# An output product in 64x64 TensorE quadrants, with single scores in a new plan

## The chip, the cores and the metric

One core of a Trainium2 chip. The metric is the device time of one execution in microseconds (us); "before" and "changed" are medians of several runs of the same rounds.

## The reference, cut to what matters

Attention with normalised q and k over 8 batches, 12 heads, 448 tokens and head size 64; then a feed-forward layer on the 3584 tokens.

```python
q_n, k_n = rmsnorm(q, g_q), rmsnorm(k, g_k)
attn = softmax(q_n @ k_n.T / 8)                 # per batch and head
x = (attn @ v) as 3584 x 768
h = x @ w_in                                    # 768 -> 2048
g = h + sin(alpha * h) ** 2 / alpha
out = g @ w_out                                 # 2048 -> 768
```

## The kernel before

Each batch b has a stage: its 21 score tiles (S), the attention of its 6 head pairs (A), and, as filler for TensorE (F), the output product of batch b - 1. A stage ends with the first product (x @ w_in, tile `hps`), which fills g_sb. Stages 1 to 7 are the ones with fillers. `ops`, `sc`, `av` and `hps` are PSUM tiles; there are four *bank pairs*, and all of them share these.

```python
def bank_pair(name, dtype=F32):          # one of four slots of two PSUM banks
    slot = min(free_at, key=free_at.get) # the slot that a rough clock expects first
    ...
def second_product(b):
    ...
    units = [[(i, half) for half in range(2)] for i in order]   # one row tile: both halves of 768 columns
    ...                                                         # batch 0 and odd batches differ: cut here
    for unit in units:
        def step(m, unit=unit, st=st):
            if m == 0:
                st["ps"] = bank_pair("ops")
            for k, (i, half) in enumerate(unit):
                ...                                             # c0: first column of this row tile
                nc.tensor.matmul(st["ps"][:, k, :HALF], g_sb[:, m, c0:c0 + P],          # 128x128
                                 w_out_sb[:, m, half * HALF:(half + 1) * HALF], start=(m == 0), stop=(m == MT - 1))
            if m == MT - 1:
                nc.vector.tensor_copy(osb[:, :n], st["ps"][:, :n, :HALF])
                ...                                                                    # store
# ... one stage:
PLAN = "6 SS 7 SS 7 SSS 8 SSS 8 SSAS 7 SS 5 SSASA 4 S 4 SSAAA"    # 6 fillers, 2 scores, 7 fillers, ...
SLOTS = 24                                  # the plan's 83 entries in 24 slots
at[2] += [lambda: begin_norm(n3), step_of(n3, 0, 1, 2)]            # next batch's norm: squares on GpSimd
at[10] += [lambda: begin_norm(n4), step_of(n4, 0, 1)]
for slot, task in ((10, step_of(n3, 3)), (11, step_of(n3, 4)),     # two sums on VectorE (reduce)
                   (12, step_of(n3, 5)), (12, step_of(n4, 2)),     # inverse root on ScalarE, then scaling
                   (13, step_of(n4, 3)), (15, step_of(n4, 4)), (17, step_of(n3, 6)), (18, step_of(n4, 5)),
                   (23, step_of(n4, 6))):
    at[slot].append(task)
```

`attend` (A) ends with a logarithm and an exponential on ScalarE (tile `rec`) and two VectorE multiplies into `xT`, which give its bank pair back. Scores give theirs back after ScalarE's exponential (`expT`). An output unit gives its pair back after VectorE's copy into `osb`.

Of the kernel before, what the change touches and what calls it, by code (L numbers as in the profile page):

```python
# [23 lines left out]
F32 = mybir.dt.float32  # L24
# [8 lines left out]
def kernel(  # L33
# [23 lines left out]
    nc = tc.nc  # L57
    B, H, S, D = q.shape
    D_MODEL = H * D
    D_FF = moe_w_in.shape[1]  # L60
    P = 128
    KT = D_MODEL // P
    MT = D_FF // P
    NP = H // 2
    NT = S // P
    REST = S - NT * P
    NJ = S // REST
# [3 lines left out]
    HALF = D_MODEL // 2  # L71
# [16 lines left out]
    opool = ctx.enter_context(tc.tile_pool(name="osb", bufs=3))  # L88
# [8 lines left out]
    def bank_pair(name, dtype=F32):  # L97
        slot = min(free_at, key=free_at.get)
        clock["pe"] = max(clock["pe"], free_at.pop(slot))
        ps = psum.tile([P, 2, 2048 // mybir.dt.size(dtype)], dtype, tag=f"ps{slot}", name=name)  # L100
        slot_of[id(ps)] = slot
        return ps

    def passes(pe=0.0, act=0.0):

        clock["pe"] += pe
        if act:
            clock["act"] = max(clock["act"], clock["pe"] + 0.25) + act
        return max(clock["pe"], clock["act"] if act else 0.0)

    def give_back(ps, time):
        free_at[slot_of.pop(id(ps))] = time
# [48 lines left out]
    w_out_sb = wpool.tile([P, MT, D_MODEL], BF16)  # L161
    g_sb = gpool.tile([P, MT, 2 * S], BF16)
# [222 lines left out]
    def second_product(b):  # L385


        steps = []
        odd = b % 2
        rows = [out[c * S:(c + 1) * S, :].rearrange("(p j) d -> j p d", j=NJ) for c in range(B)]  # L390
        order = [NT] * odd + list(range(NT))

        units = [[(i, half) for half in range(2)] for i in order]
        if b == 0:
            units = [[(i, half) for i in rows_] for half in range(2) for rows_ in (order[:2], order[2:])]
        if odd:
            units[-1:] = [[x] for x in units[-1]]
        for unit in units:
            st = {}

            def step(m, unit=unit, st=st):
                if m == 0:
                    st["ps"] = bank_pair("ops")
                for k, (i, half) in enumerate(unit):
                    c0 = odd * (S + REST) + i * P if i < NT else NT * P
                    nc.tensor.matmul(st["ps"][:, k, :HALF], g_sb[:, m, c0:c0 + P],  # L406
                                     w_out_sb[:, m, half * HALF:(half + 1) * HALF], start=(m == 0), stop=(m == MT - 1))
                passes(0.163 * len(unit))
                if m == MT - 1:
                    n = len(unit)  # L410
                    osb = opool.tile([P, 2, HALF], F32, tag="osb", name="osb")
                    nc.vector.tensor_copy(osb[:, :n], st["ps"][:, :n, :HALF])  # L412
                    give_back(st["ps"], passes() + 1.2)
                    whole = n == 2 and unit[0][0] == unit[1][0]
                    for k, (i, half) in enumerate(unit[:1] if whole else unit):
                        src = osb.rearrange("p a d -> p (a d)") if whole else osb[:, k]
                        cols = slice(0, D_MODEL) if whole else slice(half * HALF, (half + 1) * HALF)
                        for jj in range(2):
                            dst = rows[b][odd + 2 * i + jj] if i < NT else rows[b - 1 + jj][(NJ - 1) * (1 - jj)]
                            eng = nc.scalar if b == B - 1 and jj else nc.sync  # L420
                            eng.dma_start(out=dst[:, cols], in_=src[jj * 64:jj * 64 + 64, :])
            each = 2 // len(unit)
            steps += [lambda m=m, s=step, e=each: [s(m * e + x) for x in range(e)] for m in range(MT // each)]
        return steps
# [9 lines left out]
    c0, c1 = norm[0], norm[1]  # L434
# [108 lines left out]
    first_product(0, beside)  # L543


    PLAN = "6 SS 7 SS 7 SSS 8 SSS 8 SSAS 7 SS 5 SSASA 4 S 4 SSAAA"
    KEPT, SLOTS = MT // 2, 24
    plan = [x for word in PLAN.split() for x in ("F" * int(word) if word.isdigit() else word)]
    for b in range(1, B):
        nc.scalar.preload_act_table_set(EXP_LN)  # L550
        clock["act"] = clock["pe"] + 3.3
        fillers.extendleft(reversed(second_product(b - 1)))

        n_fill = len(fillers) - (KEPT if b % 2 == 0 else 0)
# [30 lines left out]
    for s in second_product(B - 1):  # L585
        s()
# [28 lines left out]
```

## Time and profile before

| | before |
|---|---|
| time | 434.88 us |
| TensorE busy | 98% |
| ScalarE, GpSimd, VectorE busy | 78%, 64%, 53% |
| stage 1 (from the end of hps to the next hps) | 30.44 us |
| stages 2 to 7, each | 32.02 us |

A "stage" below is always the stretch from the modelled end of one batch's hps matmuls to the start of the next batch's. It is the best yardstick here: stages 2 to 6 of a kernel agree within 0.03 us where the clock is the same, while the time to the first hps differs between runs (38.2 to 41.3 us, with how many half-clock stretches fall in it).

### The profile page before, as it was taken

The numbers are of one execution on the slowest core, as the hardware profiler recorded it, in microseconds if no ns is written. First come the engines' busy times: TensorE is split into PE (matmuls) and PEld (weight loads), VectorE is DVE, ScalarE is ACT, GpSimd is POOL, SyncE is SP. The second block draws the span as 40 slices with busy tenths as digits, with TensorE's granted clock in tenths as the row PEclk, the third lists the DMA queues.
The fourth block names the chain that finished last, engine by engine and source line by source line (L and its number), as shares of the span: only waits on it lengthen the run. The fifth ranks groups of instructions, "written<-read, shape, count | busy, mean of one in ns | idle before, by whom it ended". The sixth has DMA issues, their size and how long they took to land.

```text
span 434.6 us, 9514 instructions
## 1 busy us (share of the span) xinstructions
PE 423.9 (98%) x3844; PEld 220.5 (51%) x3844; DVE 231.6 (53%) x335; ACT 338.4 (78%) x529; POOL 279.7 (64%) x263
## 2 busy tenths in 40 slices
PE   7889999999999999999999999999999999999996
PEld 3335554555455555555555555555555555555563
DVE  4778564557455564547453564464645474246511
ACT  4889789878888787878879788887878788788600
POOL 4969789936995659927798369947599176002300
PEclk9989999999999999999999999999999999999999
DMA  7999999690249505692067903494063901320022
GB/s 254 209 257 206 215 192 231 143 267 15 67 151 217 144 0 131 121 223 100 10 193 180 194 1 82 150 221 125 1 196 85 126 1 33 84 57 2 0 67 79
DMA packets 68240, 54.63 MB, mean 126 GB/s; under 512 B 39636, under 2 KB 63972, under 8 KB 68196
## 3 DMA queue, kind: packets, MB, share of 16 engines
q1 hardware_dynamic: 54834, 40.51, 36.1%
q0 software_dynamic: 12416, 11.81, 18.0%
q10 hardware_dynamic: 946, 1.70, 1.0%
q8 instruction: 30, 0.49, 0.5%
q14 instruction: 14, 0.11, 0.1%
HBM read 45.62 MB, written 11.01 MB: 130 GB/s over the span
## 4 chain that ended last, share of the span: by engine, by line
PE 82%; DVE 1%; ACT 1%; POOL 0%; issue 0%; POOLq 0%
PE ops L406 32%; PE hps L353 29%; PE av L314 13%; PE sc L294 7%; ACT expT L297 1%; DVE ms L227 0%; POOL sq L221 0%; DVE osb L412 0%; DVE g_sb L340 0%; DVE xT L326 0%; ACT inv L236 0%; ACT inv L237 0%; POOLq L246 0%
## 5 line engine op out<-in xcount | busy, mean ns | idle before, releaser
L297 ACT ACTIVATE expT<-sc 128x896 bf16<-128x896 f32 x168 | 144.7, 914 | 30.6 <-PE sc L294 29.5
L406 PE MATMUL ops<-w_out_sb,g_sb 128*128 128x384 bf16 x896 | 156.6, 327 | 0.0
L353 PE MATMUL hps<-xT,w_in 128*128 128x448 bf16 x768 | 146.8, 353 | 0.0
L335 POOL TENSOR_TENSOR s<-s 128x448 f32<-128x448 f32 x64 | 59.5, 934 | 114.4 <-ACT s L332 100.8
L406 PEld LDWEIGHTS <-g_sb 128*128 128x128 bf16 x896 | 83.1, 98 | 70.0 <-issue 18.8
L340 DVE SCALAR_TENSOR_TENSOR g_sb<-s,inv_alpha_sb,hps 128x448 bf16<-128x448 f32 x128 | 80.8, 676 | 60.9 <-POOL s L335 60.9
L353 PEld LDWEIGHTS <-w_in 128*128 128x128 bf16 x768 | 74.4, 98 | 71.4 <-issue 2.9
L332 ACT ACTIVATE s<-hps,alpha_sb 128x448 f32<-128x448 f32 x128 | 74.6, 628 | 28.3 <-PE hps L353 26.5
L326 DVE TENSOR_TENSOR xT<-av,rec 64x448 bf16<-64x448 f32 x96 | 59.7, 622 | 50.1 <-ACT rec L321 30.8
L246 POOL TENSOR_TENSOR qkn<-qk,inv 128x448 bf16<-128x448 f32 x80 | 72.7, 939 | 7.4 <-POOL qk L224 7.0
L221 POOL TENSOR_TENSOR sq<-qk 128x896 f32<-128x896 f32 x44 | 73.4, 1685 | 0.0
L314 PE MATMUL av<-expT,vb 64*64 64x448 bf16 x672 | 70.6, 352 | 0.6 <-DVE osb L412 0.3
L314 PE MATMUL av<-expT,ones 64*64 64x448 bf16 x672 | 70.7, 352 | 0.0
L227 DVE TENSOR_REDUCE ms<-sq 128x14 f32<-128x896 f32 x44 | 47.5, 1083 | 25.0 <-POOL sq L221 24.7
L412 DVE COPY osb<-ops 128x768 f32<-128x768 f32 (+1 forms) x33 | 27.6, 837 | 51.4 <-PE ops L406 45.5
L294 PE MATMUL sc<-qkT 64*64 64x448 bf16 x672 | 51.3, 362 | 2.5 <-DVE qkT L276 1.4
L224 POOL TENSOR_TENSOR qk<-qk,gg 128x896 f32<-128x896 f32 x24 | 50.2, 2094 | 1.8 <-ACT gg L171 1.8
L314 PEld LDWEIGHTS <-vb 64*64 64x64 bf16 x672 | 37.6, 107 | 12.5 <-issue 1.1
L314 PEld LDWEIGHTS <-ones 64*64 64x64 bf16 x672 | 37.4, 107 | 11.3
L337 ACT ACTIVATE s<-s 128x448 f32<-128x448 f32 x64 | 36.9, 577 | 2.8
L294 PEld LDWEIGHTS <-qkT 64*64 64x64 bf16 x672 | 15.1, 105 | 30.6 <-issue 26.4
L321 ACT ACTIVATE rec<-rec 128x448 f32<-128x448 f32 x48 | 27.7, 577 | 1.5
(44 smaller groups left out, 138.6 us busy)
## 6 DMA issues: line engine op xcount, KB each, us to landing
qk<-in_q_dram SPq DMA_DIRECT2D x24, 448.0 KB, 4.8
qk<-in_k_dram SPq DMA_DIRECT2D x22, 448.0 KB, 4.8
out_dram<-osb SPq DMA_DIRECT2D x39, 192.0 KB, 2.8
vb<-in_v_dram POOLq DMA_DIRECT2D x32, 168.0 KB, 6.4
w_in<-in_moe_w_in_dram POOLq DMA_DIRECT2D x4, 768.0 KB, 11.9
w_out_sb<-in_moe_w_out_dram POOLq DMA_DIRECT2D x2, 1536.0 KB, 24.2
out_dram<-osb SPq DMA_DIRECT2D x26, 96.0 KB, 4.5
qk<-in_k_dram ACTq DMA_DIRECT2D x2, 448.0 KB, 6.0
```

The source lines that it names most:

```text
L221: nc.gpsimd.tensor_mul(st.sq[w], qk[ci][:, w], qk[ci][:, w])
L224: eng.tensor_mul(qk[ci][:, 0], qk[ci][:, 0], gg.to_broadcast([P, 2 * NJ, D]))
L246: eng.tensor_mul(n[:, :, hi, :], x[:, hi], inv[:, hi].unsqueeze(2).to_broadcast([P, NJ, D]))
L294: nc.tensor.matmul(sc[key_rows(pp, hi), pp, :S], qkt[r, 1, j * REST:(j + 1) * REST], qkt[r, 0, :], start=True, stop=True)
L297: nc.scalar.activation(expT[c, j], sc[:, :, :S], ACT.Exp, scale=SCALE)
L314: nc.tensor.matmul(av[o, part, :S], ones[r, :] if part else vb[b][r, hp, j, :], expT[pi // 2, j][r, pi % 2, :], start=(j == 0), stop=(j == ...
L326: nc.vector.tensor_mul(xT[b][r, hp, :], av[r, 0, :S], rec[o, :])
L332: nc.scalar.activation(s1, hps, ACT.Sin, scale=alpha_sb[:, m, :])
L335: nc.gpsimd.tensor_mul(s2, s1, s1)
L340: nc.vector.scalar_tensor_tensor(g_sb[:, m, (b % 2) * S:(b % 2 + 1) * S], s2, inv_alpha_sb[:, m, :], hps, op0=ALU.mult, op1=ALU.add)
L353: nc.tensor.matmul(ps[:, m % 2, :S], w_in_sb[m * 2 // MT][:, kt, m % (MT // 2) * P:(m % (MT // 2) + 1) * P], x[:, kt, :], start=(kt == 0), ...
L406: nc.tensor.matmul(st["ps"][:, k, :HALF], g_sb[:, m, c0:c0 + P], w_out_sb[:, m, half * HALF:(half + 1) * HALF], start=(m == 0), stop=(m == ...
```

## The change

Its intent: run the output product in 64x64 quadrants, the shape of scores and attention, so that TensorE does not change shape within a stage; then scores need not be bunched. A quadrant contracts 64 rows, so each output exists as two halves in two banks: VectorE copies one and adds the other. A unit is now one half of the columns of a row tile, and it takes a whole bank pair, as a unit of both halves did before. Batch 7's product stays as it was.

```diff
-        units = [[(i, half) for half in range(2)] for i in order]
+            units = [[(i, half)] for i in order for half in range(2)]       # batches 1 to 6; batch 0 half by half
...
+            def quadrants(m, unit=unit, st=st):
+                for r in range(2):
+                    for o in range(2):
+                        rs, os = slice(r * 64, r * 64 + 64), slice(o * 64, o * 64 + 64)
+                        nc.tensor.matmul(st["ps"][os, r, :HALF], g_sb[rs, m, c0 + o * 64:c0 + o * 64 + 64],
+                                         w_out_sb[rs, m, half * HALF:(half + 1) * HALF], start=(m == 0), stop=(m == MT - 1))
+                if m == MT - 1:
+                    nc.vector.tensor_copy(osb[:, 0], st["ps"][:, 0, :HALF])
+                    nc.vector.tensor_add(osb[:, 0], osb[:, 0], st["ps"][:, 1, :HALF])
...
+            step = whole_array if b == B - 1 else quadrants
...
-    PLAN = "6 SS 7 SS 7 SSS 8 SSS 8 SSAS 7 SS 5 SSASA 4 S 4 SSAAA"
+    PLAN = "6 S 4 S 2 S 2 S 2 S 2 S 2 SS 2 S 2 A 1 S A 3 S 2 S 2 S 2 S 1 S 1 S 4 S A S A 3 S 2 S 5 S 4 AA 2"
```

More of the change, by code (lines that the diff above doesn't have):

```diff
@@ L391, in second_product, with store, whole_array @@
         order = [NT] * odd + list(range(NT))
-        units = [[(i, half) for half in range(2)] for i in order]
-        if b == 0:
-            units = [[(i, half) for i in rows_] for half in range(2) for rows_ in (order[:2], order[2:])]
-        if odd:
-            units[-1:] = [[x] for x in units[-1]]
+        if b == B - 1:
+            units = [[(i, half) for half in range(2)] for i in order[:-1]] + [[(order[-1], half)] for half in range(2)]
+        elif b == 0:
+            units = [[(i, half)] for half in range(2) for i in order]
+        else:
+            units = [[(i, half)] for i in order for half in range(2)]
+        osbs = {}
+        def store(osb, i, cols):
+            for jj in range(2):
+                dst = rows[b][odd + 2 * i + jj] if i < NT else rows[b - 1 + jj][(NJ - 1) * (1 - jj)]
+                eng = nc.scalar if b == B - 1 and jj else nc.sync
+                eng.dma_start(out=dst[:, cols], in_=osb[jj * 64:jj * 64 + 64].rearrange("p a d -> p (a d)"))
         for unit in units:
             st = {}
-            def step(m, unit=unit, st=st):
+            def whole_array(m, unit=unit, st=st):
                 if m == 0:
@@ L409, in step @@
                 if m == MT - 1:
-                    n = len(unit)
+                    n, i = len(unit), unit[0][0]
                     osb = opool.tile([P, 2, HALF], F32, tag="osb", name="osb")
@@ L413, in step @@
                     give_back(st["ps"], passes() + 1.2)
-                    whole = n == 2 and unit[0][0] == unit[1][0]
-                    for k, (i, half) in enumerate(unit[:1] if whole else unit):
-                        src = osb.rearrange("p a d -> p (a d)") if whole else osb[:, k]
-                        cols = slice(0, D_MODEL) if whole else slice(half * HALF, (half + 1) * HALF)
-                        for jj in range(2):
-                            dst = rows[b][odd + 2 * i + jj] if i < NT else rows[b - 1 + jj][(NJ - 1) * (1 - jj)]
-                            eng = nc.scalar if b == B - 1 and jj else nc.sync
-                            eng.dma_start(out=dst[:, cols], in_=src[jj * 64:jj * 64 + 64, :])
+                    store(osb[:, :n], i, slice(unit[0][1] * HALF, (unit[-1][1] + 1) * HALF))
+            def quadrants(m, unit=unit, st=st):
+                (i, half), = unit
+                if m == 0:
+                    st["ps"] = bank_pair("ops")
+                c0 = odd * (S + REST) + i * P if i < NT else NT * P
+                for r in range(2):
[3 more added lines that the diff above has]
+                                         w_out_sb[rs, m, half * HALF:(half + 1) * HALF], start=(m == 0), stop=(m == MT - 1))
+                passes(0.163)
+                if m == MT - 1:
+                    if half == 0 or b == 0:
+                        osbs[i] = opool.tile([P, 2, HALF], F32, tag="osb", name="osb")
+                    osb = osbs[i][:, half:half + 1]
+                    nc.vector.tensor_copy(osb[:, 0], st["ps"][:, 0, :HALF])
+                    nc.vector.tensor_add(osb[:, 0], osb[:, 0], st["ps"][:, 1, :HALF])
+                    give_back(st["ps"], passes() + 1.6)
+                    apart = b == 0 or (odd and i == order[-1])
+                    if apart:
+                        store(osb, i, slice(half * HALF, (half + 1) * HALF))
+                    elif half:
+                        store(osbs[i], i, slice(0, D_MODEL))
+            step = whole_array if b == B - 1 else quadrants
             each = 2 // len(unit)
```

## The prediction

> **What bounds the kernel now.** I read the page's busy shares and its chain first, then the chain in order of time, the stretches of one batch, and the timelines of ScalarE, VectorE and GpSimd inside one attention stage.
>
> ```profile
> PE 423.9 (98%) x3844; PEld 220.5 (51%) x3844; DVE 231.6 (53%) x335; ACT 338.4 (78%) x529; POOL 279.7 (64%) x263
> PEclk9989999999999999999999999999999999999999
> PE 82%; DVE 1%; ACT 1%; POOL 0%; issue 0%; POOLq 0%
> ```
>
> TensorE is busy nearly always, at full clock, and 82% of the chain that ended last is TensorE work. A busy TensorE is not a TensorE at its best, though, so the chain in order of time comes next. This is the attention stage of batch 2, with the products around it:
>
> ```profile
> 107.71 1.95 PE ops L406 x12
> 109.66 0.50 PE sc L294 x8
> 110.16 2.38 PE ops L406 x14
> 112.54 0.50 PE sc L294 x8
> 113.04 2.38 PE ops L406 x14
> 115.42 0.69 PE sc L294 x12
> 116.11 2.71 PE ops L406 x16
> ...
> 122.72 1.32 PE av L314 x28
> 124.04 0.19 PE sc L294 x4
> 124.23 2.38 PE ops L406 x14
> ...
> 135.82 3.97 PE av L314 x84
> 139.79 18.27 PE hps L353 x96
> ...
> 409.82 20.81 PE ops L406 x128
> ```
>
> The last line gives the price of the output product alone: 20.81 us / 128 = 0.1626 us a pass (384 columns). Two lines above it, av in 64x64 quadrants, four matmuls together, takes 3.97 us / 21 groups = 0.189 us a group (448 columns). A whole-array pass of the same 448 columns (hps) takes 18.27 / 96 = 0.190. So four quadrants together cost what one whole pass costs. A score group (4 quadrant matmuls) between two av groups takes 0.19. But between output passes two score groups take 0.50 and not 0.38, and 14 output passes take 2.38 and not 2.28. Each excursion from 128x128 to 64x64 and back costs about 0.12 + 0.10 us.
>
> The sum confirms it. The stage from 107.7 to 139.8 lasts 32.1 us and holds 112 output passes, 21 score groups and 42 av groups: 112 x 0.1626 + 63 x 0.189 = 18.21 + 11.91 = 30.12. What is over is 1.98 us. The plan has nine runs of output passes, each followed by scores or attention, so nine round trips: **0.22 us a round trip**, with nothing left for waits. In these stages TensorE never waits; its only waste is the change of shape.
>
> Next, what stands close behind TensorE:
>
> ```profile
> 107.70:139.80 32.10, 32.10 (x366) 16.83 (x364) 15.83 (x22) 27.43 (x41) 26.96 (x24) 1.00 0.53 137
> 139.80:158.06 18.26, 18.26 (x98) 9.43 (x99) 11.41 (x18) 14.31 (x24) 9.69 (x9) 1.00 0.44 103
> ```
>
> The columns after the span are TensorE, weight load, VectorE, ScalarE, GpSimd. In the stage ScalarE works 27.4 of 32.1 us: second bound, 4.7 us of slack. GpSimd 27.0, VectorE 15.8.
>
> ```profile
> L297 ACT ACTIVATE expT<-sc 128x896 bf16<-128x896 f32 x168 | 144.7, 914 | 30.6 <-PE sc L294 29.5
> L412 DVE COPY osb<-ops 128x384 f32<-128x384 f32 x10 | 5.6, 558 | 8.1 <-PE ops L406 8.0
> L412 DVE COPY osb<-ops 128x768 f32<-128x768 f32 x23 | 22.0, 958 | 43.3 <-PE ops L406 37.4 <-DMA qkT<-qkn 5.8
> ```
>
> The exponentials wait for scores, 29.5 us in all, and not the other way round.
>
> [...]
>
> **The change part by part.**
> Removed: the shape change between output passes, scores and attention. In each of the seven stages (batches 1 to 7, which carry the output products of batches 0 to 6) nine round trips become one, from and to hps. Gain 8 x 0.22 = 1.77 us a stage, 12.4 us over seven.
>
> Added on TensorE: the 768 whole passes of batches 0 to 6 become 3072 quadrant matmuls, with as many weight loads. A group of four should cost 384 columns as one pass does, 0.1626 us, by the av comparison. Two things could spoil that. A quadrant's weight load lasts 107 ns, which still fits under a 160 ns stream. Eight instructions in 162 ns are 20 ns each; av does eight in 189 (24 ns), and the PE transposes of the first stage do 224 instructions in 3.6 us (16 ns each). So neither binds. [...]
>
> Added on VectorE: per row tile, two copies and two adds of 384 columns in place of one copy of 768. A copy is 0.558; the add I estimate at 0.56 from the same size (the xT multiply of 448 columns is 0.62). That is 4 x 0.56 - 0.96 = 1.3 us, times 24 row tiles = 31 us more on VectorE, 232 to 263 of about 425. In the stage some 16 + 4.5 = 20.5 of 30 us: beside TensorE, not in its way, except that a bank pair comes back after 1.2 us and not 1.0, and there are twice as many bank pairs (7 units a stage, not 3.5) out of four.
>
> Moved: the scores, from bunches of two and three to singles every two filler steps (0.65 + 0.19 = 0.84 us). ScalarE takes an exponential every 0.80 us when they follow each other (three in 2.51 us in its timeline). So TensorE now offers them at the rate ScalarE can take. I walked the plan by hand with F = 0.325, S = 0.189, A = 1.323 us from the stage's start; ScalarE is free for the first exponential at 3.1 us (table load and sines before it, 110.82 - 107.7). Scores 5 to 9 are issued at 6.1, 6.9, 7.8, 7.9 and 8.8; exponentials 3 to 7 end at 6.2, 7.0, 7.8, 8.6 and 9.4, each giving a slot back. With one pair for the running output unit and one being drained after the 16th step (until about 7.4 us), score 6 waits about 0.15 us and the next unit's first step 0.05. The walk finds similar crumbs at the later unit ends (24, 32, 48), about 0.3 us in all. ScalarE ends its last exponential near 26.7 us and the last reciprocal at 30.7, while TensorE ends at 30.3. Both are nearly level, so **I charge 0.3 us a stage for waits**.
>
> The first stage is another matter: it lasts 31.7 us with only 96 output passes (15.6 + 11.9 + 2.0 = 29.5 expected), because VectorE stands behind late squares on GpSimd (sq at 72.9 to 76.2, VectorE idle 2.6 us before its sum) and attention waits for xT. That wait of 2.2 us is not of the shape change, and the new plan reaches the same point no later. I give this stage 1.2 us of gain, not 1.77.
>
> Sum: 434.75 - 6 x (1.77 - 0.3) - 1.2 = 424.7, which I round to **424.6 us**, 2.3% less.
>
> **The rivals.** (a) *ScalarE becomes the bound.* Its 27.4 us of work must fit in 30.35, after a start 3.1 us late; GpSimd and VectorE feed its small inverses. For it: the walk shows ScalarE busy without a gap from 3.1 to 14 us. Against: it idles 29.5 us before exponentials now. If each stage lost 1 us to it, the time would be 434.75 - 12.4 + 7 = 429.4, within 2%. (b) *Bank pairs come back late.* VectorE works in order: a copy stands behind a multiply that waits for a reciprocal (2 to 3 us of VectorE idle at three such places in the stage), and now twice as many units depend on it. If two of the seven units in a stage cost 0.4 us each: 428. (c) *A quadrant group costs more than a pass* (weight loads of the same row half, row halves in two banks). At 170 ns the loss is 7.5 ns x 768 = 5.8 us, and the time 430. Against it stands av. (d) *Nothing is lost*: no waits, and the first stage gains fully: 422.4; if the first stage also loses its old wait, 420.5.
>
> **Range and chances.** The floor is (d), 421 to 422; (a), (b) and (c) reach 428 to 430, and I don't expect two of them at once. Range 421.8 to 429.0. The border of 2% lies at 426.1, 1.5 us above my number, that is 0.2 us a stage. So faster 0.66, within 2% 0.31, slower 0.03; slower would need a new wait of 3 us in every stage.
>
> **What would show it right or wrong.** In the chain in order of time, score groups between output groups should take 0.19 and not 0.25 to 0.31, and output groups 0.162. The stage between two hps runs should be 30.4 to 30.8 us (32.1 now), the first 30.5. VectorE busy should be about 263 us, ScalarE's idle before expT well below 29.5. If TensorE shows waits for ScalarE (score slots) or for VectorE (output slots) of more than 0.5 us a stage, rival (a) or (b) has it; if output groups take 170 ns without waits, (c). The prediction is wrong at its root if the stage keeps 32 us although the round trips are gone.

That the halves need a copy and then an add, and not one instruction, is not shown here; it is how the change is written.

## The result

Before 434.88 us, changed 450.18 us (449.24 to 452.53). The ratio is 1.036 (95% interval 1.033 to 1.039): slower by 3.6%. Ratios are the mean time of one kernel's fast runs over that of the other's of the same rounds, so not quite the ratio of the medians quoted. The profiled run took 452.53 us, the slowest of the five, at a granted clock of 0.98; the others had 0.985 to 0.989, so its stages hold more of the half clock told of below than those of the median run.

The page of the changed kernel:

```profile
PE 425.1 (94%) x6148; PEld 264.1 (59%) x6148; DVE 259.6 (58%) x403; ACT 338.2 (75%) x529; POOL 280.0 (62%) x263
PEclk9889999999989999899999999999998999999999
```

TensorE, busy 98% before, now waits, and its clock is below full speed in several slices. But the quadrants themselves do as predicted. The chain in order of time, stage 2, first lines:

```profile
117.65 0.65 PE ops L435 x16
118.30 0.19 PE sc L294 x4
```

Sixteen quadrant matmuls, four groups, take 0.65 us, 0.1625 each (0.1626 for a whole pass before), and a score group between them takes 0.19 (0.25 before). The shape change is gone. A copy takes 556 ns and an add 554, as estimated. So the loss is in waits. The stages of the changed kernel, of batches 2, 4 and 7, in windows set by hand that are up to 0.04 us longer than the stages in the table below (span, TensorE, weight load, VectorE, ScalarE, GpSimd; then the granted clock):

```profile
113.36:148.20 34.84, 32.69 (x702) 24.17 (x702) 19.44 (x31) 28.05 (x42) 27.02 (x24) 0.95 0.52 117
219.94:253.40 33.46, 31.21 (x702) 23.08 (x702) 19.45 (x31) 27.84 (x42) 27.02 (x24) 1.00 0.46 122
376.89:407.70 30.81, 30.57 (x702) 22.44 (x702) 15.30 (x27) 26.98 (x38) 6.60 (x6) 1.00 0.29 56
```

The last stage carries the same quadrants and the same plan and is 1.2 us shorter than before (30.77 against 32.02). What it lacks is the norm of a next batch: four sums on VectorE (31 to 27 instructions) and GpSimd's work for them. The other stages are longer than before, and those in which the clock fell are longer by another 1.4 to 1.7 us (34.8 to 35.1 against 33.4). Here is the chain in stage 2 where it leaves TensorE:

```profile
123.53 1.35 PE av L314 x27
...
129.78 1.10 DVE ms L227
...
130.90 0.33 ACT inv L236
...
131.48 0.81 ACT expT L297
...
132.33 0.56 PE sc L294 x4
132.89 0.64 PE ops L435 x8
```

A score group waits for an exponential (a bank pair), which stands behind the norm's inverse on ScalarE, which waits for a sum on VectorE. The last line shows the clock: eight quadrant matmuls take 0.64 us and not 0.33. VectorE in the same stretch, the changed kernel:

```profile
126.09 1.26 DVE L326 TENSOR_TENSOR xT<-av,rec 64x448 bf16<-64x448 f32 x2 [1.37 <-ACT rec L321]
127.38 1.08 DVE L227 TENSOR_REDUCE ms<-sq 128x14 f32<-128x896 f32 x1
128.50 1.25 DVE L326 TENSOR_TENSOR xT<-av,rec 64x448 bf16<-64x448 f32 x2
129.78 2.08 DVE L227 TENSOR_REDUCE ms<-sq 128x14 f32<-128x896 f32 x2
131.89 0.56 DVE L442 COPY osb<-ops 128x384 f32<-128x384 f32 x1
132.48 0.55 DVE L443 TENSOR_TENSOR osb<-osb,ops 128x384 f32<-128x384 f32 x1
```

and the kernel before, at the same place in its stage 2:

```profile
117.78 1.09 DVE L227 TENSOR_REDUCE ms<-sq 128x14 f32<-128x896 f32 x1 [2.67 <-POOL sq L221]
119.42 1.09 DVE L227 TENSOR_REDUCE ms<-sq 128x14 f32<-128x896 f32 x1 [0.56 <-POOL sq L221]
120.95 0.96 DVE L412 COPY osb<-ops 128x768 f32<-128x768 f32 x1 [0.44 <-PE ops L406]
123.12 1.08 DVE L227 TENSOR_REDUCE ms<-sq 128x14 f32<-128x896 f32 x1 [1.20 <-POOL sq L221]
125.39 1.26 DVE L326 TENSOR_TENSOR xT<-av,rec 64x448 bf16<-64x448 f32 x2 [1.18 <-ACT rec L321]
```

Before, three of the sums stand ahead of the first multiplies into xT, with idle time of VectorE around them. In the new plan the multiplies of pair 0, which wait for a reciprocal, stand ahead of all three, and those of pair 1 ahead of the last two; sums, multiplies, copy and add form one chain of 6.9 us without a gap (126.09 to 133.0), and three bank pairs hang on it. (The profile puts 12 us of VectorE's idle time before copies down to stores of `osb`. One such copy, at 123.58, began 0.05 us after the last matmul of its unit, 122.88 + 0.65, so no store held it up.)

### The profile page after: what moved, and what is told of

It reads as the page before. It is cut to its first block, busy times and chain, and to the rows that moved or that the text cites. A ratio compares the mean times of both kernels' runs of the same rounds, so it can differ in the third digit from the quotient of the medians.

```text
span 450.8 us, 14156 instructions
## 1 busy us (share of the span) xinstructions
PE 425.1 (94%) x6148; PEld 264.1 (59%) x6148; DVE 259.6 (58%) x403; ACT 338.2 (75%) x529; POOL 280.0 (62%) x263
## 4 chain that ended last, share of the span: by engine, by line
PE 64%; DVE 9%; ACT 7%; POOL 3%; issue 2%; POOLq 0%
PE hps L353 25%; PE ops L435 19%; PE av L314 10%; PE sc L294 5%; PE ops L415 5%; ACT expT L297 4%; DVE ms L227 3%; DVE g_sb L340 3%; DVE xT L326 3%; POOL s L335 3%; ACT rec L321 1%; ACT rec L320 1%; ACT s L332 1%; ACT inv L236 0%; ACT inv L237 0%
## 5 line engine op out<-in xcount | busy, mean ns | idle before, releaser
L435 PE MATMUL ops<-w_out_sb,g_sb 64*64 64x384 bf16 x3072 | 161.2, 330 | 3.5 <-DVE g_sb L340 1.7
L435 PEld LDWEIGHTS <-g_sb 64*64 64x64 bf16 x3072 | 104.2, 109 | 40.6 <-issue 6.4
L294 PE MATMUL sc<-qkT 64*64 64x448 bf16 x672 | 68.3, 363 | 14.6 <-ACT expT L297 9.8
L314 PE MATMUL av<-expT,vb 64*64 64x448 bf16 x672 | 73.3, 354 | 0.7 <-ACT expT L297 0.4
L314 PE MATMUL av<-expT,ones 64*64 64x448 bf16 x672 | 73.0, 354 | 0.0
L442 DVE COPY osb<-ops 128x384 f32<-128x384 f32 x48 | 26.7, 556 | 41.6 <-PE ops L435 29.1
L314 PEld LDWEIGHTS <-vb 64*64 64x64 bf16 x672 | 42.0, 109 | 9.1 <-issue 1.3
L314 PEld LDWEIGHTS <-ones 64*64 64x64 bf16 x672 | 41.8, 109 | 7.9
L294 PEld LDWEIGHTS <-qkT 64*64 64x64 bf16 x672 | 26.7, 108 | 30.8 <-issue 22.4
L320 ACT ACTIVATE rec<-av 128x448 f32<-128x448 f32 x48 | 26.0, 541 | 20.8 <-PE av L314 20.5
```

What stands on the lines that cost most here:

```text
L294: nc.tensor.matmul(sc[key_rows(pp, hi), pp, :S], qkt[r, 1, j * REST:(j + 1) * REST], qkt[r, 0, :], start=True, stop=True)
L314: nc.tensor.matmul(av[o, part, :S], ones[r, :] if part else vb[b][r, hp, j, :], expT[pi // 2, j][r, pi % 2, :], start=(j == 0), stop=(j == ...
L435: nc.tensor.matmul(st["ps"][os, r, :HALF], g_sb[rs, m, c0 + o * 64:c0 + o * 64 + 64], w_out_sb[rs, m, half * HALF:(half + 1) * HALF], star ...
```

## The experiments

Stages in us, from the profiled run, and the median time of all runs; a profiled run lies up to 2.4 us from its median. "h" marks values that hold a stretch at half clock.

| kernel | stage 1 | stages 2 to 6 | stage 7 | time |
|---|---|---|---|---|
| before | 30.44 | 32.02 | 32.02 | 434.88 |
| changed | 34.43 | 33.42; 34.8 to 35.1 h | 30.77 | 450.18 |
| quad_old_plan | 33.49 | 31.29 | 30.81 | 433.68 |
| whole_new_plan | 37.07 h | 35.99 | 34.80 | 464.33 |
| sums_early | 33.39 | 31.88 | 30.77 | 436.03 |
| two_units | 35.87 h | 33.94; 35.6 h | 31.26 | 455.48 |
| quad_old_sum16 | 33.44 | 31.18 | 30.81 | 433.23 |
| quad_old_no_add | 31.80 | 30.73 | 30.73 | 429.68 |
| inv_late | 36.74 h | 32.87 | 30.76 | 444.07 |
| quad_1to6_sum16 | 30.44 | 31.18 | 30.80 | 431.03 |
| new_no_add | 36.01 | 33.45; 35.0 h | 30.77 | 447.93 |
| sums_no_add | 32.76 | 31.30 | 30.76 | 433.63 |
| first_unit_m13 | 30.44 | 31.18 | 30.81 | 431.10 |
| first_tile_whole | 31.47 | 31.80 | 31.42 | 435.69 |

The kernel before took 435.09 us beside the first four, 436.15 beside the next four (434.9 to 436.5) and 434.92 beside the last four.

**One part each: the plan or the quadrants.**

```diff
# quad_old_plan, from the changed kernel        # whole_new_plan, from the kernel before
-    PLAN = "6 S 4 S 2 S ..."                   -    PLAN = "6 SS 7 SS ..."
+    PLAN = "6 SS 7 SS ..."                     +    PLAN = "6 S 4 S 2 S ..."
```

> The quadrants kept, the plan of before put back. Theory A (the quadrants do what was predicted, the new plan's order does the harm: it puts the attention of pairs 0 and 1 ahead of the sums of the next batch's norm, VectorE reaches the sums late, ScalarE stands in its inverse and TensorE runs out of score slots): 424 to 428 us, every stage near 30.5 to 31 us, with at most 0.5 us of wait for g_sb at a stage's start. Rival B (the quadrants do the harm: twice as many bank pairs and 31 us more of VectorE): 440 us or more, the stage stays at 33 or above.

> The kernel before with the new plan alone: whole-array output product, 21 runs of output passes a stage and not 9. The shape changes alone cost 12 x 0.22 = 2.6 us a stage, 18 us in all: 453 us. Theory A adds the wait behind the sums, 1.5 to 3 us in six stages: 462 to 471 us, with ScalarE waiting about 2 us a stage for the sums before its inverse. Rival B: no such wait, 453 us.

quad_old_plan: 433.68 us, ratio 0.997 (0.994 to 0.999). whole_new_plan: 464.33 us, ratio 1.067 (1.064 to 1.070). The first falls between the two theories: the plan does most of the harm, but the quadrants do not give 424 either. The second is theory A's number, and its stages tell how it is made up. In stage 7, without sums, it is 34.80 - 32.02 = 2.78 us longer than before: twelve more round trips at 0.23. In stages 2 to 6 it is 3.97 longer, so there 1.2 us more are of the plan's order. With quadrants the order costs 33.42 - 31.29 = 2.1 us in stages 2 to 6 and nothing in stage 7 (30.77 against 30.81). So where there is no next norm, single scores cost nothing. Rival (a) of the prediction, ScalarE as the bound, finds no support there; sums_no_add below tests it with the norm present.

What is left in quad_old_plan is VectorE again, smaller. Its stage 2, VectorE and then the chain:

```profile
127.87 1.09 DVE L227 TENSOR_REDUCE ms<-sq 128x14 f32<-128x896 f32 x1
128.99 0.56 DVE L442 COPY osb<-ops 128x384 f32<-128x384 f32 x1
129.58 0.55 DVE L443 TENSOR_TENSOR osb<-osb,ops 128x384 f32<-128x384 f32 x1
```

```profile
129.58 0.56 DVE osb L443
...
130.18 0.57 PE sc L294 x8
```

A score waits 0.5 us for an output unit's bank pair, because the sum stands ahead of the copy. Stage 1 lost 3.05 us, most of it at such places (TensorE waits there four times for an add: 0.7, 0.7, 1.6 and 0.8 us).

**The sums ahead of the multiplies.**

```diff
+        sums = {33: step_of(n3, 3), 36: step_of(n3, 4)} if b + 1 < B else {}   # entries of the plan, just ahead of A, A
-            for slot, task in ((10, step_of(n3, 3)), (11, step_of(n3, 4)), (12, step_of(n3, 5)), ...
+            for slot, task in ((12, step_of(n3, 5)), ...
```

> The changed kernel with two sums of the norm moved on VectorE: the first just ahead of the attention of pair 0, the second just ahead of that of pair 1. Theory A: ScalarE's wait for the sums (2.1 us a stage) and TensorE's waits of 0.6 and 1.9 us and the half clock after them go: stage near 31 us, 428 to 432 us in all. Rival B: nothing moves, 448 us or more. Rival C (ScalarE can't follow single scores anyway): the wait moves elsewhere, 440 to 446 us.

436.03 us, ratio to before 1.002 (1.000 to 1.004): 14 us less than the changed kernel with two sums moved, and no half clock in any stage. Stages 2 to 6 fell from 33.42 to 31.88 us without half clock, which makes 7.7 us for the five; stage 1 gave 1.0, and most of the rest is the half clock that no longer comes. Theory A's direction, but its 31 us and 428 to 432 were not reached. VectorE, stage 2 of this run:

```profile
123.35 1.09 DVE L227 TENSOR_REDUCE ms<-sq 128x14 f32<-128x896 f32 x1
124.47 1.26 DVE L326 TENSOR_TENSOR xT<-av,rec 64x448 bf16<-64x448 f32 x2
125.76 1.08 DVE L227 TENSOR_REDUCE ms<-sq 128x14 f32<-128x896 f32 x1
126.87 0.56 DVE L442 COPY osb<-ops 128x384 f32<-128x384 f32 x1
```

One of the sums now stands ahead of the first multiplies (at 120.61, they at 122.06), so that one fewer stands between these and the copy; the rest of the chain is still there.

**Whether ScalarE's standing is enough.**

```diff
-                               (11, step_of(n3, 4)), (12, step_of(n3, 5)), ...
+                               (11, step_of(n3, 4)), (14, step_of(n3, 5)), ...       # the inverse two slots later
```

> The changed kernel with the norm's inverse of the next batch's first group moved on ScalarE to two slots later, the sums on VectorE left where they are. If ScalarE, standing in that inverse for the sums, is what starves TensorE: ScalarE's 2.1 us go, stage 31.5 us or less, 432 to 437 us. If VectorE holding the output unit's and the attention's bank pairs is enough by itself: stage 33 us or more, 442 us or more.

444.07 us, ratio 1.019 (1.016 to 1.022): 6 us less than the changed kernel. ScalarE's wait for the sum fell from 2.1 to 0.4 us a stage, but the stage fell only from 33.42 to 32.87, 2.8 us over five stages; most of the rest goes with the half clock, which in the profiled run fell in stage 1 alone. The chain of this run now leaves TensorE for VectorE alone:

```profile
129.04 2.08 DVE ms L227 x2
...
131.15 0.57 DVE osb L442
...
131.74 0.56 DVE osb L443
...
132.35 0.38 PE sc L294 x4
```

So ScalarE standing in the inverse is the last link, not the cause: without it the same score waits 1.6 us for the output unit's pair. The cause is the place of the sums in VectorE's order. (The limit of 33 us that I had set for this case was missed by 0.13.)

**VectorE's added work.** The add left out, wrong results on purpose:

```diff
-                    nc.vector.tensor_add(osb[:, 0], osb[:, 0], st["ps"][:, 1, :HALF])
```

> Quadrants with the old plan, the add of the second bank left out (the result is wrong on purpose): VectorE has 27 us less, and each bank pair comes back 0.58 us earlier. Theory A: the wait of 0.47 us in stages 2 to 6 goes (2.4 us), and of the 3.05 us that the first stage lost some 1.5 to 2: 429 to 430 us. If VectorE's added work does not matter: 433.7 us.

> The changed kernel with the add of the second bank left out (wrong on purpose): VectorE 27 us less, each output bank pair back 0.58 us earlier. If the order of the sums in the new plan does its harm by itself, the wait behind them stays: stages of 32.2 to 32.9 us without the half clock, 441 to 447 us. If the harm is only VectorE's added time: 436 us or less.

> The new plan with the two sums moved ahead (436.0 us, stages of 31.87) and the add left out as well (wrong on purpose). If the rest over the ideal stage is VectorE's added time plus 0.45 us for g_sb at the start: stages of 30.8 us, 429 to 431 us, as quadrants with the old plan and no add (429.7). If single scores cost something of their own: 433 us or more.

With the old plan 429.68 us, ratio 0.986 (0.983 to 0.988): stages 2 to 6 at 30.73, the same as stage 7, and stage 1 down by 1.7. With the new plan as it is 447.93, and 33.45 us against 33.42: nothing gained. (Its first stage even grew, from 34.43 to 36.01 us: a score there waits 1.9 us, until 68.57, for a transposed q and k from DMA, `qkT<-qkn`, a wait that the changed kernel does not have. Why this transfer came late was not followed.) With the sums moved 433.63 us, 31.30 against 31.88. So the add costs 0.56 to 0.58 us a stage where the order is good, and is hidden behind the sums where the order is bad. The expectation for the last run, 30.8, was missed, and its 433.63 us fall under "single scores cost something of their own". Its trace says otherwise. In stage 4 an output unit waits 0.48 us for the bank pair of the early multiplies, where in quad_old_no_add a score waits 0.21 behind these multiplies, and the start waits 0.43 us for g_sb against 0.29; no wait for an exponential is over 0.08 us. These make 0.5 of the 0.57 us between 31.30 and 30.73. So the rest is again the early attention in VectorE's order, and not ScalarE. (These waits are counted from the steady pace of the matmuls, 0.0406 us a quadrant of output; by the same count the changed kernel has 0.48 and 0.43 us at the two places.)

**The start of a stage.** The changed kernel wants g_sb of m 14 after 14 groups, half as late as before; it waits 0.47 us at 116 us. Two ways to take that away. In two_units the first two units run abreast; in first_unit_m13, built on the fastest version, the first unit reads older rows. Its output is wrong, which doesn't matter for the time.

```diff
# two_units, from the changed kernel
+            steps[:16] = steps[:7] + steps[8:15] + [steps[7], steps[15]]
# first_unit_m13, from quad_1to6_sum16
+                gm = m - 2 if first and m > 13 else m       # g_sb[rs, gm, ...]
```

> The changed kernel with the first two output units of a stage run abreast, so that the last two k-steps (g_sb of m 14 and 15) are wanted after 28 groups and not after 14. Theory A says that only the 0.5 to 0.8 us at each stage's start goes: 3 to 6 us less than the changed kernel, 444 to 447 us. If the wait at the start is what puts the later waits where they are, 435 us or less.

> The fastest version so far (431.0 us), the first output unit of a stage taking m 12 and 13 of g_sb again in place of 14 and 15 (wrong on purpose), so that it does not wait for the end of the first product's tail. If the wait at the start is worth its 0.45 us: six stages 31.18 to 30.73, 428.3 us. If the time comes back in later waits for bank pairs: 431 us.

two_units: 455.48 us, ratio 1.046 (1.044 to 1.049) where the changed kernel had 1.036: slower still, and both expectations missed. Two pairs for output units at once leave two for scores: in its stage 3 TensorE waits 0.4 and 0.6 us for exponentials at the start, and the later waits (0.5 and 1.9 us) are all still there. first_unit_m13: 431.10 us, stages of 31.18 us as without it. The first unit no longer stops for g_sb, which had cost 0.29 us in quad_1to6_sum16 and not the 0.45 expected. But the second unit then waits 0.16 us, put down to the same last instruction of g_sb, and a score behind it 0.24 us and not 0.09, its weight load for the first unit's add. So the gain was not to be had: bank pairs, by the trace, are what is short.

**Versions meant to be faster.**

```diff
# quad_old_sum16, from quad_old_plan: one sum after the copy and the add
-                               (13, step_of(n4, 3)), (15, step_of(n4, 4)), ...
+                               (13, step_of(n4, 3)), (16, step_of(n4, 4)), ...
# quad_1to6_sum16: the same, and batch 0 on the whole array with its units and stores of before
+            step = whole_array if b in (0, B - 1) else quadrants
# first_tile_whole, from quad_1to6_sum16: first row tile of each stage on the whole array
+            units = [[(order[0], half) for half in range(2)]] + [[(i, half)] for i in order[1:] for half in range(2)]
+    PLAN = "8 SSS 8 SS 6 SS 6 SSS 8 SSAS 7 SS 5 SSASA 4 S 4 SSAAA"
```

> Quadrants with the old plan (433.7 us, stages of 31.29 us), one sum of the norm moved on VectorE from ahead of an output unit's copy and add to after it. Theory A (bank pairs come back late because VectorE, in order, has sums and multiplies ahead of the copy and the add): TensorE's wait of 0.47 us for the add in each of five stages goes, stages of 30.8 us, 431.2 us. Rival D (the wait is only of the added VectorE time, wherever it stands): 433.7 us still.

> A version meant to be faster than both: the output product of batch 0 as in the kernel before (whole array, in the first stage, which lost 3.05 us with quadrants), quadrants for batches 1 to 6, the old plan, and the sum moved as in the run beside it. Theory A: first stage 30.4, stages 2 to 7 at 30.8 us: 434.9 - 6 x 1.2 = 427.7 us, 427 to 429. If the first stage's loss is not of the quadrants: 430 us or more.

> The same version with the first row tile of every stage on the whole array (both halves abreast, m 14 wanted after 28 passes) and the scores of the first words set so that only one more round trip of 0.22 us is paid. No wait for g_sb (0.45 us less), 1.3 us less of VectorE: stages of 30.6 to 31.0 us, 427 to 430 us. If the start is tight for another reason, 431 us or more.

quad_old_sum16: the long wait for the add is gone, but the stage gained only 0.11 us of the 0.5, and 433.23 us is nearer to rival D than to theory A. Two waits appeared elsewhere: 0.3 us at the last three A and 0.07 at a score. quad_1to6_sum16: 431.03 us, ratio 0.988 (0.986 to 0.991), correct, faster than both kernels, though by less than the 2% that count as faster here. The 427 to 429 us expected were not reached, since stages 2 to 6 stayed at 31.18. Its first two stages:

```profile
57.73:88.17 30.44, 29.82 (x349) 15.73 (x347) 15.28 (x21) 27.24 (x41) 28.01 (x25) 1.00 0.99 206
106.50:137.68 31.18, 31.07 (x702) 22.07 (x701) 19.74 (x32) 27.43 (x41) 26.97 (x24) 1.00 0.56 137
```

The first stage is back at 30.44, so all of its 3.05 us were of the quadrants there, with the units and stores that go with them (the moved sum alone left 33.44 in quad_old_sum16). first_tile_whole failed: 435.69 us and 31.80 us a stage. It pays one more round trip of 0.22 us and bunches three scores at the start; in its stage 4 the output unit after the first five scores waits 0.6 us (until 216.07) for the bank pair of an exponential.

## Why the prediction was wrong

The price list was right: 0.22 us a round trip (whole_new_plan: 0.23), 0.1625 us a quadrant group, 0.55 us a copy or an add, VectorE 259.6 us busy (263 said). Rivals (a) and (c), which it held for less likely, did not come true. Where nothing else happens, in stage 7, the walk's 30.4 to 30.8 us came out: 30.77.

**The step that failed is "I charge 0.3 us a stage for waits"**, and the hand walk behind it. The walk followed TensorE and ScalarE and gave VectorE a fixed 1.2 us per bank pair. VectorE kept to the order of the program here: it stood idle for 1.37 us until 126.09 for the reciprocal, though the squares of two sums had been done at 125.04, and the first of these sums came behind the multiplies, at 127.38 us; from 126.09 to 133.0 us each instruction ran behind the other. The walk did not ask what the two early A put in front of the sums of slots 10 and 11. Measured in their place, stage 4, without half clock, against 30.6 said: about 2.9 us of waits more. The gaps between TensorE's matmuls in stage 2, which has the same ones, are 0.47 us (g_sb at the start), 0.59 (an output unit for a bank pair that the multiplies hold) and 1.88 (a score behind the sum and the inverse).

**Rival (b) came closest, and was sized at 428.** It had the engine and its order right, but named only multiplies that wait for reciprocals, not the sums behind them. It was written as "If two of the seven units in a stage cost 0.4 us each"; the waits in stage 2 cost 0.59 and 1.88 us. Nor did it count what a bank pair carries: a unit of one half of the columns (384) now holds the pair that two halves (768) shared, until a copy and an add of 0.556 + 0.554 us, where one copy of 0.958 us had freed it.

**The clock was left out.** The 1.88 us of idle TensorE, which came 0.65 us of work after the 0.59, was followed in three of five stages of the profiled run by 3.4 us at a granted clock of 0.5, worth 1.4 to 1.7 us each: 4.8 us. The forecast had no term for it. Why three and not five? In the traces of both kernels all changes of the granted clock lie on a grid of 3.41 us (in the changed kernel half clock from 132.42 to 135.83, 187.03 to 190.44 and 344.04 to 347.46). The stretches of this grid just before the half clock had 1.5 to 1.6 us of matmuls (stages 2, 3 and 6). In stages 4 and 5 a border of the grid cut the same idle time in two, and no stretch had under 2.0 us. This is a hint and no rule: a stretch of stage 1 with 1.5 us was followed by full clock.

**"The new plan reaches the same point no later" for stage 1** failed too: 4.0 us longer than before and not 1.2 shorter. Quadrants with the old plan lose 3.05 of it; quad_1to6_sum16 gets it back. That stage has 48 fillers and not 56 between its scores, so that its pairs are probably wanted sooner; this was not tested. The prediction had also misread the stage: 31.7 us with a wait of 2.2. By the yardstick here it took 30.44 us, with two waits of 0.5 us (until 66.31 and 79.13), so there was less to gain. (Smaller slips: in the stage of batch 2 VectorE idles for over 2 us before multiplies at two places, 2.17 and 2.57 us, not at three; 434.75 - 12.4 - 2.2 is 420.2, not 420.5. They change nothing.)

The sum for the profiled run: stage 1 5.2 us over the prediction, stages 2 to 6 together 19.1 (5 of it the clock), stage 7 0.2, and 1.7 before the first hps, where two stretches of half clock fell and one in the kernel before.

Settled is that the order of the sums makes this a loss: with two of them moved the time is that of the kernel before (sums_early, 1.002). It does not bring the gain; the new plan with the sums moved is still 11 us over the prediction. Settled too is that leaving out the add saves about 0.57 us a stage where the order is not in the way. Open are why stage 1 suffers more than the others, and why the late transfer in new_no_add was late.

## What to carry to other kernels

When a plan is rearranged, write down the order of work of every engine, not only of the bound one: a task that keeps its place in the plan changes its place in an engine's work when something else moves across it (here the sums, behind multiplies that waited until 126.09 us). Splitting the contraction over row halves halved what a PSUM bank pair carries here (384 columns and not 768); with four pairs for everything, count how long each is held before counting what the bound engine saves. And read a stage that lacks one ingredient (here the last, without a next norm): it told from a single trace that the quadrants and the single scores cost nothing as long as the norm's work is away (30.77 us against 32.02 before).
